# Chunk-selected attention with a gated feed-forward: query rows and their selection by DMA from the second pair on, two more engine choices, a shorter load count in the planner, and new ranks

## The chip, the cores and the metric

The kernel runs on one core of one Trainium2 chip. The metric is device microseconds per execution. For the kernel before it is the median of three runs, 320.1 us (319.93 to 320.34). The chip's engines each run their own instruction queue in order: TensorE (PE, with PEld for its weight loads), VectorE (DVE), ScalarE (ACT), GpSimd (POOL), and SyncE (SP), which here only issues DMAs.

## The reference

Inputs q, k, v have shape (4, 8, 768, 64) in fp32. Keys fall into 24 chunks of 32. For each query an upper bound of its score against each chunk is computed from the chunk's minimum and maximum, the six best causal chunks are kept, and attention runs over those alone. The result, as 3072 rows of 512, goes through a normalised SwiGLU feed-forward (512 to 1536 to 512).

```python
k_min = np.min(k_chunks, axis=3);  k_max = np.max(k_chunks, axis=3)
ub = np.sum(np.maximum(q[:, :, :, None, :] * k_min[:, :, None, :, :],
                       q[:, :, :, None, :] * k_max[:, :, None, :, :]), axis=-1)
ub = np.where(causal, ub, -1000000000.0)
top_chunks = np.argsort(ub, axis=-1)[..., -top_k:]             # top_k = 6
...
scores = np.where(mask, scale * np.matmul(q, k.transpose(0, 1, 3, 2)), -1000000000.0)
attn = softmax(scores)                                          # then attn @ v
...
rms = np.sqrt(np.mean(x * x, axis=-1, keepdims=True) + 1e-06)
xn = x / rms * rms_g
g = xn @ w_gate
return (g * (1.0 / (1.0 + np.exp(-g))) * (xn @ w_val)) @ w_out
```

## The kernel before, in words

The unit of the attention part is a pair of heads: 16 pairs, four to a batch (`for p in range(NPAIRS)`). For a pair, `prep` loads keys and queries (`kload`, `qload`, line 504, on SP), turns them so that the head dimension lies on partitions (`kT`, `qT`, TensorE in fp32, line 526), copies them out of PSUM (`kE`, `qE`), takes each chunk's maximum and minimum (`kmx`, `kmn`, VectorE, lines 552 and 554) and their difference (`dif`, line 633), rectifies the queries (`relu`, line 666), and forms the bounds (`ub`, line 684). The bounds are copied out, turned back (`up`, line 708), masked (`ubm`), and the eight largest of each row are found (`max`, line 729). `pick` (step `sel`) then writes 24 flags and an offset per query and head. Flags and queries together are the right operand of the score matmul, QS, where rows 0 to 63 of one head are the queries and rows 64 on the selection; KE holds keys and a fixed pattern E, so one matmul gives scores in which unselected chunks are pushed far down.

QS is filled in one of two ways, by the constant `QM`. For pairs below `QM` (0 to 3 before), the turned queries are cast into QS (`qC`, two casts of 64x768), `pick` writes a tile `selq` with two instructions (lines 748 and 753), TensorE turns it (`selT`, line 768, six matmuls), and two copies bring it out of PSUM (`selC`). For pairs from `QM` on (`side_q`), the untransposed queries are cast into a row tile QN (`qN`, one cast of 128x768), `pick` writes the flags into the same tile with two instructions for each head (lines 739 and 742), and two DMA transposes on SP carry the whole into QS (`qX`, line 563). There are two QN tiles (`qn=2`). Scores (line 831), exponentials (line 848) and the product with v (line 867) follow in groups; every score matmul waits for the whole selection of its pair.

When all four pairs of a batch are done, `norm` takes each half batch, three row blocks of 128 at a time: sums of squares, an inverse root on GpSimd, and a scaling of each row block (`xs`, line 944, VectorE). Batch 0 is then turned on TensorE (`tp`, line 966), the other batches by DMA transposes (line 955). `ffn` runs gate (line 1000), value (1021) and output (1041) matmuls on TensorE with tanh on ScalarE and two products on VectorE.

The order of all this is written by a planner, `Order.run`, before the kernel is built. Every piece of work is a step with an estimated duration for each engine that may do it. At each moment of planned time a free engine takes the ready step with the lowest rank, provided that its buffers are free. Ranks are sums from two tables: `RANK` (per kind, for batch 0 and for later ones) and `TIMES` (per pair or stage: `a` for preparation, `l` for loads, `s` for scores, `n` for norms, `f` for the feed-forward). A step with bytes to load is taken to arrive when the planned DMA has moved everything before it at `RATE` bytes per us, plus 1.5 us; loads are held back while the planned DMA is over 3 us behind. The resulting lists are fixed; at run time the engines follow them in order and wait on semaphores.

TensorE's idle time in the beginning is filled with matmuls on zeros: 48 of 512 columns from the start (`BUSY`) and 40 of 256 columns after pair 2's scores (`LATER`), as steps with rank 1000 and more (line 345):

```python
for i in range(BUSY):
    bank = Buf("ps")
    add("busy", "PE", pe(4 * P), 1000.0 + i, busy(bank, 4 * P), [c_zero], opens=[bank])
```

`ROWS` and (after) `KSIDE` equal 16, the number of pairs, so the branches that they guard for the keys run in neither kernel.

Of the kernel before, what the change touches and what calls it, by code (L numbers as in the profile page):

```python
# [8 lines left out]
FP32 = mybir.dt.float32  # L9
# [18 lines left out]
        av=132.14, dif=-438.04, eps=7.54, exp=-319.11, kC=334.22, kE=136.01, kT=-485.02,  # L28
        kload=-54.57, kmn=-137.23, kmx=-301.52, max=-152.41, qC=109.54, qE=316.44, qT=171.34,
        qload=-51.07, relu=59.75, root=77.15, sc=154.73, sel=83.19, selC=291.06, selT=-117.97,  # L30
        sq=-378.33, tp=24.59, tpE=360.56, ub=-188.41, ubE=-631.05, ubm=-71.86, up=-402.33,
        vload=-29.64, xb=-262.2, xs=247.58,
    ),
    dict(
        av=-265.86, dif=4.6, eps=-792.39, exp=258.27, gate=4.29, hh=-241.0, kC=134.04,
        kE=332.01, kT=-79.45, kload=194.09, kmn=455.81, kmx=359.92, mask=48.28, max=274.06,
        out=-113.88, po=207.1, poE=221.55, qE=-270.87, qN=298.48, qT=-27.26, qX=-362.48,
        qload=199.51, relu=279.63, root=-878.4, sc=-37.49, sel=336.13, sq=111.91, tanh=315.81,
        tg=61.58, ub=88.65, ubE=-137.69, ubm=107.32, up=172.52, val=34.42, vload=256.19,
        xT=-70.38, xb=-239.74, xs=-343.95,  # L40
# [38 lines left out]
class Order:  # L79
    RATE = 0.2e6  # L80
# [17 lines left out]
    def run(self, places):  # L98
# [20 lines left out]
        while len(out) < len(self.steps):  # L119
# [6 lines left out]
            for e in free:  # L126
# [3 lines left out]
                for s in waiting[e]:  # L130
# [71 lines left out]
def kernel(  # L202
# [78 lines left out]
    def act(n):  # L281
        return 0.065 + n * 0.00083
# [113 lines left out]
    if ROWS < B * NP:  # L396
# [89 lines left out]
    def prep(c, i0, nb, at, lr):  # L486
# [6 lines left out]
        done, ready = {}, {}  # L493
        rows_k, side_q = p >= ROWS, p >= QM
        for w, src in (("k", k), ("q", q)):
# [20 lines left out]
            if w == "k" and rows_k:  # L516
                continue

            evs = []
            for j0 in range(0, nb, 3):  # L520
                bank = Buf("ps", "prep")

                def turn(e, w=w, j0=j0, bank=bank):
                    t = tile_of(bank, [P, 3 * P], FP32, "p" + w)
                    for j in range(3):
# [5 lines left out]
                         opens=[bank], uses=[nat[w]])  # L531

# [38 lines left out]
        if rows_k:  # L571
            kh, km, kt = Buf("kh"), Buf("km"), Buf("ps", "prep")

            def load_h(e):
                t = tile_of(kh, [QC, 2, CH // 4, D], FP32, "khalf")
                for h in range(2):
                    nc.sync.dma_start(out=t[:, h], in_=k[b, h0 + h].rearrange(
                        "(c t) d -> c t d", t=CH // 4))

            ldh = add("khload", "SP", 1.4, rank(lr, b, "khload"), load_h, opens=[kh], load=220000)  # L580

            def whole(e, which):
                op = ALU.min if which else ALU.max
                if not which:
                    tile_of(km, [QC, 2, CH // 8, D], FP32, "kmm")
                to, src = (kh if which else km).tile, kh.tile
                m = CH // 8
                while m:
                    nc.vector.tensor_tensor(out=to[:, :, 0:m], in0=src[:, :, 0:m],
                                            in1=src[:, :, m:2 * m], op=op)  # L590
                    src, m = to, m // 2

            w_x = add("kmx", "DVE", 1.15, rank(at, b, "kmx"), lambda e: whole(e, 0), [ldh], opens=[km],
                      uses=[kh])
            w_n = add("kmn", "DVE", 1.15, rank(at, b, "kmn"), lambda e: whole(e, 1), [w_x], uses=[kh])

            def turn_m(e):
                t = tile_of(kt, [P, 2, QC], FP32, "kmt")
                for m, x in ((0, km), (1, kh)):
                    nc.tensor.transpose(t[:, m], x.tile[:, :, 0, :], ident_f[0:QC, 0:QC])  # L600

            tmt = add("kT", "PE", 0.19, rank(at, b, "kT"), turn_m, [w_x, w_n, c_id], opens=[kt],
                      uses=[km, kh])

            def join(e):
                tile_of(mx, [P, NCH], FP32, "kmx")
                for m in range(2):
                    nc.vector.tensor_reduce(
                        out=KU[c.ku.slot][:, 0, 0:NCH] if m else mx.tile[:],
                        in_=kt.tile[:, m].rearrange("p (c t) -> p c t", t=4),  # L610
                        axis=AXX, op=ALU.min if m else ALU.max)

            reds.append(add("join", "DVE", 0.44, rank(at, b, "join"), join, [tmt] + c_ku,
                            opens=[mx, c.ku], uses=[kt]))
# [27 lines left out]
        for w, dst in (("k", KE), ("q", QS)):  # L642
            if rows_k if w == "k" else side_q:
                continue
# [19 lines left out]
        def relu(e):  # L664
            t = tile_of(rel, [P, S], FP32, "rt")
            nc.vector.tensor_scalar(out=t[:, 0:n], in0=big["q"].tile[:, 0:n], scalar1=0.0,
                                    scalar2=None, op0=ALU.max)
# [436 lines left out]
```

## Time and profile before

| | |
|---|---|
| median of 3 runs | 320.1 us (319.93 to 320.34) |
| the profiled execution | 320.69 us, span 319.0 us, granted TensorE clock 0.998 |
| TensorE busy | 312.6 us, 98% of the span |
| VectorE, ScalarE, GpSimd busy | 237.2 (74%), 189.7 (59%), 105.1 (33%) us |
| DMA | 34.98 MB moved, 110 GB/s over the span |

The span runs from the first instruction to the last. Busy time is a sum over instructions and says nothing of which one ends last; the chain of waits, followed back from the last instruction, does. Matmul ends are modelled, so a busy TensorE may still contain short waits. Line numbers (L768) are those of the kernel before.

### The profile page before, as it was taken

The numbers are of one execution on the slowest core, as the hardware profiler recorded it, in microseconds if no ns is written. First come the engines' busy times: TensorE is split into PE (matmuls) and PEld (weight loads), VectorE is DVE, ScalarE is ACT, GpSimd is POOL, SyncE is SP. The second block draws the span as 40 slices with busy tenths as digits, with TensorE's granted clock in tenths as the row PEclk, the third lists the DMA queues.
The fourth block names the chain that finished last, engine by engine and source line by source line (L and its number), as shares of the span: only waits on it lengthen the run. The fifth ranks groups of instructions, "written<-read, shape, count | busy, mean of one in ns | idle before, by whom it ended". The sixth has DMA issues, their size and how long they took to land.

```text
span 319.0 us, 7874 instructions
## 1 busy us (share of the span) xinstructions
PE 312.6 (98%) x2922; PEld 199.6 (63%) x2940; DVE 237.2 (74%) x684; ACT 189.7 (59%) x418; POOL 105.1 (33%) x155
## 2 busy tenths in 40 slices
PE   8999999999999999999999999999999999999995
PEld 4576887666657767775657665567666566555542
DVE  7787988999965798999997968674677978716300
ACT  4478988553318888996348465469777343323121
POOL 8768345540003647496026135114211100000000
PEclk9999999999999999999999999999999999999999
DMA  9999994899929998959973414572000430001022
GB/s 174 218 208 176 201 126 78 107 201 170 69 65 213 211 184 192 165 126 205 78 112 85 46 28 55 121 170 82 16 2 2 83 84 0 2 33 66 35 89 109
DMA packets 111702, 34.98 MB, mean 110 GB/s; under 512 B 104624, under 2 KB 108464, under 8 KB 111664
## 3 DMA queue, kind: packets, MB, share of 16 engines
q1 hardware_dynamic: 81552, 26.23, 40.2%
q0 software_dynamic: 28512, 7.87, 26.3%
q10 hardware_dynamic: 1600, 0.39, 0.6%
q8 instruction: 23, 0.38, 0.5%
q14 instruction: 15, 0.12, 0.1%
HBM read 28.57 MB, written 6.29 MB: 109 GB/s over the span
## 4 chain that ended last, share of the span: by engine, by line
PE 96%; DVE 2%; issue 1%; ACT 0%; ACTq 0%; DVEq 0%
PE vp L1021 20%; PE gp L1000 20%; PE po L1041 19%; PE sc L831 11%; PE av L867 6%; PE ub L684 5%; PE busy L345 5%; PE pk L526 4%; PE pq L526 3%; PE up L708 2%; PE sc L837 1%; PE st L768 0%; PE tp L966 0%; DVE kmx L552 0%; DVE qs L300 0%
## 5 line engine op out<-in xcount | busy, mean ns | idle before, releaser
L848 ACT ACTIVATE pt<-sc 128x512 bf16<-128x512 f32 (+3 forms) x192 | 90.1, 583 | 10.4 <-PE sc L831 8.2
L1007 ACT ACTIVATE sg<-gp 128x384 bf16<-128x384 f32 x96 | 47.3, 497 | 62.9 <-PE gp L1000 61.3
L1021 PE MATMUL vp<-xT,wv 128*128 128x384 bf16 x384 | 75.8, 326 | 0.1
L1000 PE MATMUL gp<-xT,wg 128*128 128x384 bf16 x384 | 75.2, 326 | 0.0
L1013 DVE SCALAR_TENSOR_TENSOR tg<-sg,gp 128x384 bf16<-128x384 bf16 x96 | 51.7, 549 | 23.7 <-ACT sg L1007 22.2
L1041 PE MATMUL po<-wo,hh 128*128 128x512 bf16 x272 | 66.7, 379 | 0.8
L1029 DVE TENSOR_TENSOR hh<-vp,tg 128x384 bf16<-128x384 f32 x96 | 52.1, 552 | 14.0 <-PE vp L1021 12.4
L831 PE MATMUL sc<-qs,ke 89*128 89x128 bf16 (+5 forms) x420 | 53.3, 251 | 0.1
L1021 PEld LDWEIGHTS <-wv 128*128 128x128 bf16 x384 | 36.6, 98 | 24.7 <-issue 0.4
L1000 PEld LDWEIGHTS <-wg 128*128 128x128 bf16 x384 | 36.6, 98 | 23.3
L1041 PEld LDWEIGHTS <-hh 128*128 128x128 bf16 x288 | 27.5, 98 | 28.5 <-issue 0.4
L854 POOL TENSOR_SCALAR_AFFINE_SELECT pt<-pt 128x512 bf16<-128x512 bf16 (+1 forms) x48 | 25.4, 544 | 55.2 <-ACT pt L848 55.1
L867 PEld LDWEIGHTS <-pt 128*128 128x128 bf16 x672 | 31.4, 98 | 10.7 <-issue 2.1
L867 PE MATMUL av<-vx,pt 128*128 128x65 bf16 x672 | 36.7, 194 | 0.0
L831 PEld LDWEIGHTS <-ke 89*128 89x128 bf16 (+1 forms) x420 | 30.0, 97 | 9.2 <-issue 1.4
L300 POOL CAST ke<-kt 64x768 bf16<-64x768 f32 x31 | 27.7, 895 | 14.3 <-ACT kt L296 8.1
L298 ACT ACTIVATE osb<-po 128x512 f32<-128x512 f32 x21 | 12.7, 605 | 29.3 <-PE po L1041 29.2
L345 PE MATMUL busy<-zeros 128*128 128x512 bf16 (+1 forms) x86 | 20.5, 355 | 1.4 <-DVE zeros L340 1.3
L888 DVE TENSOR_TENSOR xb<-av,rden 128x384 bf16<-128x384 f32 (+1 forms) x34 | 18.1, 534 | 1.2
L944 DVE SCALAR_TENSOR_TENSOR xs<-xb,ri,gains 128x512 bf16<-128x512 bf16 x24 | 17.6, 766 | 1.7 <-DMA xT<-xs 1.7
L729 DVE MAX8 m<-ubm 128x8 f32<-128x24 f32 x192 | 18.7, 169 | 0.1
L633 POOL TENSOR_TENSOR ku<-kmx,ku 128x24 f32<-128x24 f32 x9 | 3.2, 357 | 45.4 <-DVE ku L554 42.8
(77 smaller groups left out, 322.3 us busy)
## 6 DMA issues: line engine op xcount, KB each, us to landing
out_dram<-osb SPq DMA_DIRECT2D x24, 256.0 KB, 2.2
knat<-in_k_dram SPq DMA_DIRECT2D x30, 192.0 KB, 4.4
qnat<-in_q_dram SPq DMA_DIRECT2D x30, 192.0 KB, 4.3
vx<-in_v_dram POOLq DMA_DIRECT2D x16, 192.0 KB, 7.1
wg<-in_moe_w_gate_dram POOLq DMA_DIRECT2D x2, 768.0 KB, 7.2
wv<-in_moe_w_val_dram POOLq DMA_DIRECT2D x2, 768.0 KB, 7.4
wo<-in_moe_w_out_dram POOLq DMA_DIRECT2D x2, 768.0 KB, 12.9
ke<-e_all SPq DMA_DIRECT2D x4, 96.0 KB, 3.7
```

The lines of the kernel that those rows point to most:

```text
L300: engine[e].tensor_copy(out_, in_)
L345: nc.tensor.matmul(t[:, 0:n], zeros[:, 0:P], zeros[:, 0:n], start=True, stop=True)
L831: nc.tensor.matmul(t[:, x:x + m, :].rearrange("p a b -> p (a b)"), ke[kk, kb * P:(kb + 1) * P], qs[kk, q0 * P:(q0 + m) * P], start=not tri ...
L848: nc.scalar.activation(out=t[:, 0:nn, :], in_=sc.tile[:, 0:nn, :], func=ACT.Exp, scale=SCALE)
L854: nc.gpsimd.affine_select(out=pt.tile[:, 0:nd, :], in_=pt.tile[:, 0:nd, :], compare_op=ALU.is_ge, fill=0.0, base=0, pattern=[[0, nd], [1, ...
L867: nc.tensor.matmul(av.tile[:, qi - i0, :], pt.tile[:, x, :], VX[c.v.slot][:, hl * NT + kb, :], start=(begin and m == 0), stop=(left[0] == ...
L1000: nc.tensor.matmul(t[:], wg[:, g, hs], XT[b].tile[:, g, cols], start=(g == 0), stop=(g == NP - 1))
L1007: nc.scalar.activation(out=t[:], in_=gp.tile[:], func=ACT.Tanh, scale=0.5)
L1013: nc.vector.scalar_tensor_tensor(out=t[:], in0=sg.tile[:], scalar=1.0, in1=gp.tile[:], op0=ALU.add, op1=ALU.mult)
L1021: nc.tensor.matmul(t[:], wv[:, g, hs], XT[b].tile[:, g, cols], start=(g == 0), stop=(g == NP - 1))
L1029: nc.vector.tensor_tensor(out=t[:], in0=vp.tile[:], in1=tg.tile[:], op=ALU.mult)
L1041: nc.tensor.matmul(po.tile[:], hhs[ht].tile[:, th * P:(th + 1) * P], wo[:, ht, :], start=(ht == 0), stop=(ht == NHT - 1))
```

## The change

Five things change together.

- `QM` goes from 4 to 1: pairs 1, 2 and 3 fill QS by the row tile and the DMA transposes, as pairs 4 to 15 already do. One `selq` tile is left of two.
- The planner may put `relu` on ScalarE as well as on VectorE.
- The planner may put `xs` on GpSimd as well as on VectorE; there it is two instructions with an fp32 tile between them. One hidden tile fewer is kept (`hh` 33 to 32).
- The planner's `RATE` goes from 0.2e6 to 0.25e6 bytes per us, and only loads over 250,000 bytes are held back.
- All values of `RANK` and `TIMES` are new.

The unused branch for keys is also written differently. The core of the diff:

```diff
 RANK = (
     dict(
-        av=132.14, dif=-438.04, eps=7.54, exp=-319.11, kC=334.22, kE=136.01, kT=-485.02,
+        av=-194.02, dif=128.57, eps=135.49, exp=-30.2, kC=211.42, kE=-32.81, kT=-200.58,
...
 TIMES = {
-    "a0": -499.17, "a1": -82.98, "a10": 213.54, "a11": 202.23, "a12": 347.75, "a13": 367.65,
+    "a0": 166.8, "a1": 73.35, "a10": 214.63, "a11": -67.16, "a12": 163.94, "a13": 312.87, "a14":
...
 class Order:
-    RATE = 0.2e6
+    RATE = 0.25e6
...
-                    if s.load and dma > t + 3.0:
+                    if s.load > 250000 and dma > t + 3.0:
                         heapq.heappush(events, dma - 3.0)
                         continue
...
-    ROWS, QM, SEL2 = 16, 4, 0.42
-    QC, HW = S // (CH // 4), NT * P + D
+    KSIDE, QM, SEL2 = 16, 1, 0.42
+    HW = NT * P + D
...
-    SLOTS = dict(ps=8, nat=7, kh=1, km=1, kb=0, qn=2, vext=4, set=3, ku=3, selq=2, qt=7, ubs=2, small=8, ubm=3,
-                 pt=10, xb=2, xt=2, row=3, xs=4, ff=8, hh=33, ob=3)
+    SLOTS = dict(ps=8, nat=7, kb=0, qn=2, vext=4, set=3, ku=3, selq=1, qt=7, ubs=2, small=8, ubm=3,
+                 pt=10, xb=2, xt=2, row=3, xs=4, ff=8, hh=32, ob=3)
...
         def relu(e):
             t = tile_of(rel, [P, S], FP32, "rt")
-            nc.vector.tensor_scalar(out=t[:, 0:n], in0=big["q"].tile[:, 0:n], scalar1=0.0,
-                                    scalar2=None, op0=ALU.max)
-
-        rl = add("relu", "DVE", 0.07 + n * 0.00056, rank(at, b, "relu"), relu, done["q"], opens=[rel],
+            if e == "ACT":
+                nc.scalar.activation(out=t[:, 0:n], in_=big["q"].tile[:, 0:n], func=ACT.Relu)
+            else:
+                nc.vector.tensor_scalar(out=t[:, 0:n], in0=big["q"].tile[:, 0:n], scalar1=0.0,
+                                        scalar2=None, op0=ALU.max)
+
+        rl = add("relu", "", {"DVE": 0.07 + n * 0.00056, "ACT": act(n)}, rank(at, b, "relu"), relu, done["q"], opens=[rel],
                  uses=[big["q"]], port=True)
...
             def scale(e, j=j, i=i, xs=xs):
                 t = tile_of(xs, [P, DM], BF16, "xs")
+                if e == "POOL":
+                    f = sb.tile([P, DM], FP32, name="xf", tag="xf")
+                    nc.gpsimd.tensor_scalar(out=f[:], in0=XB[b].tile[:, i, :], scalar1=rt.tile[:, j:j + 1],
+                                            scalar2=None, op0=ALU.mult)
+                    nc.gpsimd.tensor_tensor(out=t[:], in0=f[:], in1=gains[:], op=ALU.mult)
+                    return
...
-            x = add("xs", "DVE", 0.67, rank(at, b, "xs", j, pace), scale, [r, c_gain], opens=[xs],
+            x = add("xs", "", {"DVE": 0.67, "POOL": 1.35}, rank(at, b, "xs", j, pace), scale, [r, c_gain], opens=[xs],
                     uses=[XB[b], rt], port=True)
```

More of the change, by code (lines that the diff above doesn't have):

```diff
@@ L27 @@
     dict(
-        av=132.14, dif=-438.04, eps=7.54, exp=-319.11, kC=334.22, kE=136.01, kT=-485.02,
[L29 to L32, printed above, removed]
+        av=-194.02, dif=128.57, eps=135.49, exp=-30.2, kC=211.42, kE=-32.81, kT=-200.58,
+        kload=-56.92, kmn=138.83, kmx=-214.94, max=-121.99, qC=-64.94, qE=80.5, qN=-155.22,
+        qT=125.3, qX=-464.87, qload=-55.33, relu=54.97, root=82.86, sc=78.08, sel=-103.77,
+        selC=-123.83, selT=39.9, sq=-38.85, tp=27.84, tpE=-161.42, ub=16.24, ubE=-12.11,
+        ubm=34.91, up=-45.2, vload=-91.36, xb=123.33, xs=194.99,
     ),
     dict(
[L35 to L40, printed above, removed]
+        av=-0.69, dif=-82.23, eps=99.49, exp=34.36, gate=-20.02, hh=-151.12, kC=213.59,
+        kE=108.14, kT=-9.96, kload=-8.3, kmn=-38.66, kmx=1.9, mask=151.72, max=82.0, out=201.96,
+        po=49.59, poE=74.31, qE=-232.27, qN=3.53, qT=0.49, qX=-277.65, qload=-7.17, relu=-80.37,
+        root=-77.21, sc=22.16, sel=-4.96, sq=105.84, tanh=-255.68, tg=-113.66, ub=-57.0,
+        ubE=153.74, ubm=-146.54, up=-29.23, val=-11.61, vload=187.07, xT=101.12, xb=137.85,
+        xs=-15.06,
     ),
@@ L395 @@
     c_kb = []
-    if ROWS < B * NP:
+    if KSIDE < B * NP:
         et = Buf("ps", "prep")
@@ L492, in prep @@
         nat, big = {}, {}
-        done, ready = {}, {}
-        rows_k, side_q = p >= ROWS, p >= QM
+        done, ready, kbanks = {}, {}, []
+        side_k, side_q = p >= KSIDE, p >= QM
         for w, src in (("k", k), ("q", q)):
@@ L515, in prep @@
             ready[w] = ld
-            if w == "k" and rows_k:
-                continue
             evs = []
@@ L531, in prep @@
                          opens=[bank], uses=[nat[w]])
+                if w == "k" and side_k:
+                    kbanks.append((j0, bank, tr))
+                    continue
                 def out_(e, w=w, j0=j0, bank=bank):
@@ L570, in prep @@
         reds, casts = [], []
[L571 to L614, printed above, removed]
@@ new lines, in prep, with red2 @@
+        if side_k:
+            def red2(e, which, j0, bank):
+                a0, a1 = j0 * 4, (j0 + 3) * 4
+                if which == 0 and mx.tile is None:
+                    tile_of(mx, [P, NCH], FP32, "kmx")
+                nc.vector.tensor_reduce(
+                    out=KU[c.ku.slot][:, 0, a0:a1] if which else mx.tile[:, a0:a1],
+                    in_=bank.tile[:].rearrange("p (c t) -> p c t", t=CH), axis=AXX,
+                    op=ALU.min if which else ALU.max)
+            for j0, bank, tr in kbanks:
+                reds += [add("kmx", "DVE", 0.07 + 3 * P * 0.00106, rank(at, b, "kmx", j0, "step"),
+                             lambda e, j0=j0, bank=bank: red2(e, 0, j0, bank), [tr], opens=[mx], uses=[bank]),
+                         add("kmn", "DVE", 0.07 + 3 * P * 0.00106, rank(at, b, "kmn", j0, "step"),
+                             lambda e, j0=j0, bank=bank: red2(e, 1, j0, bank), [tr] + c_ku,
+                             opens=[c.ku], uses=[bank])]
@@ L642, in prep @@
         for w, dst in (("k", KE), ("q", QS)):
-            if rows_k if w == "k" else side_q:
+            if side_k if w == "k" else side_q:
                 continue
```

28 rows, old and new, of the table TIMES are left out of this document.

## The prediction

> **What bounds the kernel now.** I read the page first: engine shares, then the chain that ended last.
>
> ```profile
> PE 312.6 (98%) x2922; PEld 199.6 (63%) x2940; DVE 237.2 (74%) x684; ACT 189.7 (59%) x418; POOL 105.1 (33%) x155
> ...
> PE 96%; DVE 2%; issue 1%; ACT 0%; ACTq 0%; DVEq 0%
> ```
>
> TensorE carries 96% of the chain. Next I asked for stages (columns: stretch, its length, busy time and count of PE, PEld, DVE, ACT, POOL, granted clock, DMA share, GB/s), and then for the filler matmuls alone (line 345, stages from 0 to 80 us).
>
> ```profile
> 20.00:30.00 10.00, 9.91 (x138) 6.83 (x143) 8.68 (x22) 9.35 (x21) 8.02 (x10) 1.00 1.23 189
> 30.00:40.00 10.00, 10.00 (x141) 8.06 (x130) 8.37 (x39) 9.06 (x22) 4.27 (x6) 1.00 1.39 190
> 40.00:50.00 10.00, 9.85 (x170) 7.68 (x171) 8.98 (x21) 8.86 (x21) 3.41 (x6) 1.00 0.99 145
> ...
> 56.00:80.00 24.00, 24.00 (x184) 15.45 (x183) 23.41 (x76) 11.13 (x24) 7.80 (x10) 1.00 1.33 160
> ```
> ```profile
> sum 80.00, PE 20.53 PEld 8.70; mean PE 2.93 PEld 1.24
> ```
>
> From 56 us on, where the first gate matmul stands on the chain,
>
> ```profile
> 56.40 1.95 PE gp L1000 x12
> ```
>
> TensorE is full of real work. Before that it looks full too, but 20.5 us of what it does there are matmuls on zeros. These 88 fillers (48 + 40 in the code) are steps of the list like any other: every one is issued, with the change as without. So the change cannot win by "needing fewer fillers"; TensorE's total falls only by real work taken away, and any wait that the new order adds comes on top. The clock is 1.00 throughout, so it gives nothing.
>
> In one place the chain leaves TensorE for VectorE, at the fourth pair's selection (chain in order of time: start, us, what):
>
> ```profile
> 40.25 0.35 PE st L768 x6
> 40.60 0.02 issue
> 40.63 0.56 DVE qs L300
> 41.19 0.01 issue
> 41.20 0.55 DVE qs L300
> 41.75 0.34 DVE kmx L552
> ```
>
> This is exactly what the change replaces: six transposes of the selection on TensorE and two copies out of PSUM.
>
> **The change part by part.** The sum is made against the profiled execution: span 319.0, its own time 320.69, so 1.69 us lie around the span. The median shown, 320.1, is 0.59 lower; I carry the sum over to it.
>
> (1) Selection of pairs 1 to 3, rows of the old path and then of the new one (median is the middle number, ns):
>
> ```profile
> L768 PE MATMUL st<-ident_b,selq x24: 217/219/220, 18.1 to 40.4; 128*128 128x128 bf16 x24
> L748 DVE SCALAR_TENSOR_TENSOR selq<-m,ubm x4: 442/446/809, 17.2 to 38.1; 128x288 bf16<-128x288 f32 x4
> L753 DVE TENSOR_SCALAR selq<-m x4: 184/325/821, 17.5 to 38.8; 128x12 bf16<-128x12 f32 x4
> ```
> ```profile
> L739 DVE SCALAR_TENSOR_TENSOR qn<-m,ubm x24: 289/300/314, 78.8 to 214.1; 128x144 bf16<-128x144 f32 x24
> L742 DVE TENSOR_SCALAR qn<-m x24: 172/174/385, 79.0 to 214.3; 128x6 bf16<-128x6 f32 x24
> L563 SPq DMA_TRANSPOSE qs<-qn x24: 1210/1236/1971, 79.7 to 221.8; - x24
> L300 POOL CAST qn<-qnat x8: 812/822/1132, 29.5 to 212.0; 128x768 bf16<-128x768 f32 x8
> ...
> DMA to landing us min/median/max: 2.5/2.7/5.3
> ```
> ```profile
> L300 POOL CAST qs<-qt x7: 814/826/1221, 8.7 to 26.4; 64x768 bf16<-64x768 f32 x7
> L296 ACT ACTIVATE qs<-st x4: 803/804/805, 18.7 to 28.0; 64x768 bf16<-64x768 bf16 x4
> L300 DVE COPY qs<-st x4: 549/555/561, 35.8 to 41.2; 64x768 bf16<-64x768 bf16 x4
> ```
>
> TensorE loses 3 x 0.35 us (the chain's piece for six transposes) = 1.05 us, all on the path: **-1.05**. GpSimd loses six casts and gains three: 6 x 0.826 - 3 x 0.822 = 2.5 us free, off the path. ScalarE loses one pair of copies, 1.6 us; VectorE loses two pairs, 2.2 us, and its selection grows from 0.446 + 0.325 to 2 x (0.300 + 0.174), +0.18 a pair, so 1.7 us net.
>
> The latency goes the other way. For the fourth pair, from the end of line 753 to the first score matmul on line 831:
>
> ```profile
> 38.82 0.46 DVE L753 TENSOR_SCALAR selq<-m 128x12 bf16<-128x12 f32 x1
> ...
> 41.97 0.50 PE L831 MATMUL sc<-qs,ke 128*128 128x128 bf16 x6
> ```
>
> That is 41.97 - 39.28 = 2.7 us. The new link: one issue ahead (1.24), then the second transpose's landing, 2.7 at the median, 5.3 at most: 3.9 to 6.5 us, +1.2 to +3.8. Every score of a pair needs both transposes. The place is 40 us into the kernel, with the DMA share near 1; loads there land late:
>
> ```profile
> DMA packets 25247, 5.96 MB, mean 198 GB/s; under 512 B 25034, under 2 KB 25113, under 8 KB 25241
> ...
> qnat<-in_q_dram SPq DMA_DIRECT2D x12, 192.0 KB, 5.8
> ```
>
> (the DMA view of 10 to 40 us.) So I take the upper half: **+2.4** for the fourth pair, whose link stands on the chain. The second and third pairs have other pairs' work behind them and I cost them at nothing; without that cover, each costs the same again. The ends, +1.2 and +3.8, stay for the range.
>
> (2) Loads counted shorter. The planner now takes a key or query load (two issues of 192 KB, 393,216 bytes, entered as 422,400) at 422,400 / 0.25e6 = 1.69 us where it took 2.11; the chip moved 198 GB/s, so 1.99 us. The order was a little cautious and becomes 0.30 us a load optimistic; engines run it in order, so a transpose placed for an early arrival stands and everything behind it on TensorE waits. Six loads for pairs 1 to 3: between 0 and 1.8 us; I take half, **+0.9**. That loads under 250,000 no longer wait in the plan moves small issues earlier on SP; rows exist for none, and I leave it inside the second rival.
>
> (3) Rectified queries on ScalarE. Nearest rows: the same step on VectorE, a ScalarE pass over 768 columns, and the table load.
>
> ```profile
> L666 DVE TENSOR_SCALAR rt<-qt 128x768 f32<-128x768 f32 x16 | 9.4, 592 | 0.4 <-ACT qt L296 0.4
> ...
> L337 ACT ACT_TABLE_LOAD x1 | 1.3, 1283 | 3.0 <-issue 3.0
> ...
> L296 ACT ACTIVATE ke<-kt 64x768 bf16<-64x768 f32 x1 | 0.8, 841 | 0.0
> ```
>
> 0.84 on ScalarE for 0.59 on VectorE: in the early stage ScalarE is at 89 to 94%, VectorE at 84 to 90, so what moves there gains nothing; later ScalarE has room and TensorE is full. **0**, from -0.5 to +0.8 (three early ones at 0.84 less 0.59). One load of tables serves exponential, tanh and square in this trace; were the rectifier outside that set, each use would cost two loads, 2.57 us. The Trainium skill ("ScalarE: Activation LUTs", Table sets) says that cheap functions, relu among them, stand in every set; by that the cost is none, and no run so far shows it.
>
> (4) Norm rows on GpSimd. One fused VectorE instruction becomes two on GpSimd, the second with two inputs.
>
> ```profile
> L944 DVE SCALAR_TENSOR_TENSOR xs<-xb,ri,gains 128x512 bf16<-128x512 bf16 x24 | 17.6, 766 | 1.7 <-DMA xT<-xs 1.7
> ...
> L854 POOL TENSOR_SCALAR_AFFINE_SELECT pt<-pt 128x512 bf16<-128x512 bf16 x24 | 15.6, 650 | 47.8 <-ACT pt L848 47.7
> ...
> L633 POOL TENSOR_TENSOR ku<-kmx,ku 128x24 f32<-128x24 f32 x9 | 3.2, 357 | 45.4 <-DVE ku L554 42.8
> ...
> L633 DVE TENSOR_TENSOR ku<-kmx,ku 128x24 f32<-128x24 f32 x7 | 1.7, 240 | 0.0
> ```
>
> Below: two passes like line 854's, 1.30 us. Above: two VectorE passes scaled by line 633's ratio, 2 x 0.766 x 357/240 = 2.28. Planned: 1.35. I take 1.8, nearer to the upper end since two inputs are read. Three rows go on VectorE one after another ahead of the first feed-forward (3 x 0.766 = 2.3 us). With one on GpSimd the set ends at about 1.8, 0.5 earlier; with two, at 3.6, 1.3 later; with all, at 5.4, 3.1 later. Only the first set is bare, later ones lie beside a full TensorE: **+0.4**, from -0.5 to +3.1. The Trainium skill ("GPSIMD Engine Reference", Elementwise side by side) speaks against this edit: it has a two-input add at 4497 ns there against 2293 on VectorE for 2048 elements. By its figures the pair of instructions is an estimated 1.9 us and the sum 0.1 us higher; the trace shows no such instruction.
>
> (5) Relief and ranks. ScalarE and VectorE lose 1.6 and 1.7 us in the stage where both run near 90%, worth at most the larger, and VectorE stands on the chain from 40.63 us on: from -1.7 to 0, **-0.5**, since the two copies on the chain are already replaced in (1). The new ranks redo every engine's order; no row prices that. TensorE's share leaves little to gain from 56 us on and much to lose; I count it at 0 and let it widen the range. One spare hidden tile fewer (33 to 32) and one selection buffer fewer: 0, as one pair alone still uses the latter.
>
> Sum: -1.05 + 2.4 + 0.9 + 0 + 0.4 - 0.5 = +2.15 us. 320.69 + 2.15 = 322.84 for a profiled run, **322.3** for the median. Its own range is 321.0 to 325.5.
>
> **The rivals.** *Early relief decides.* If the rest of the order keeps the fourth pair off the end of the early stage (its scores behind other pairs' exponentials), the DMA link is hidden, and 1.05 us of TensorE and about 2 us of VectorE and ScalarE come off: 320.1 - 3.1 = 317.0. For it: both engines near 90%, and VectorE's place on the chain. Against it: fillers are fixed and the stage's loads saturate the DMA. It decides once the link's added 2.4 us find that much other TensorE work.
>
> *SP's queue becomes the bound.* SP issues without pause early; first and last rows of thirteen groups:
>
> ```profile
> 9.08 1.26 SPq L504 DMA_DIRECT2D knat<-in_k_dram  x2
> ...
> 34.66 3.53 SPq L504 DMA_DIRECT2D qnat<-in_q_dram  x2
> ```
>
> Six transposes add 6 x 1.24 = 7.4 us to these 29, and each stands until its selection is done, with the loads of pairs 4 to 6 behind it; both row buffers are then held till landing, and GpSimd's next layout waits with masks and casts behind it. If that runs through to TensorE: 320.1 - 1.05 + 7.4 = about 326.5. Against: those pairs are not needed before the first norm.
>
> *It comes out even:* the link's lower end (+1.2) against -1.05, the rest cancelling: 320.2. *A table load per rectifier:* three early ones, 7.7 us on ScalarE: 327.8.
>
> **How the numbers follow.** Forecast 0.46, relief 0.28, SP queue 0.15, even 0.09, table load 0.02. Slower by over 0.2% (0.64 us, about what can be told from no change): 0.63; within: 0.09; faster: 0.28. The range, 316.5 to 327.5, reaches from below the relief case to past the queue case; the ranks are its largest unknown.
>
> **What would show it.** Right: no line 768 after the first pair, three more pairs of query transposes before 60 us, landing 4 to 6 us; the chain passing through a query transpose or a load; the first gate matmul 1 to 4 us after 56.4; filler count 88 unchanged. GpSimd norm rows at 1.6 to 2.0 us the pair. One table load. Wrong: the first gate earlier than 56 us with TensorE idle no larger than now, or idle appearing behind 80 us, where I put none.

## The result, and the profile after

The changed kernel takes 335.92 us (median of six runs, 331.54 to 338.35); the kernel before took 320.22 us beside it. The ratio is 1.0445, 95% interval [1.0382, 1.0509], which is 14.2 us of 320.2 (12.2 to 16.3); it is one of means and leaves out the two longest of the six runs, so it is smaller than that of the medians. It is slower, and by far more than the 2.15 us that I had forecast. Below, each kernel is compared by its ratio, and "us" is (ratio - 1) x 320.2.

The page of the changed kernel (profiled at 335.32 us, span 333.6, granted clock 0.99), engine shares and the chain that ended last:

```profile
PE 317.5 (95%) x2922; PEld 200.5 (60%) x2922; DVE 226.8 (68%) x657; ACT 198.3 (59%) x429; POOL 141.3 (42%) x181
...
PE 73%; DMA 17%; POOL 5%; SPq 1%; issue 1%; DVE 1%; ACT 1%; ACTq 0%; DVEq 0%; POOLq 0%
```

TensorE carried 96% of the chain; now it is 73%, and DMA and GpSimd hold 22%. The span is 14.6 us longer and TensorE is busy only 4.9 us longer, so some 10 us are new idle time. The windows of the changed kernel show where (stretch, length, busy time and count of PE, PEld, DVE, ACT, POOL, granted clock, DMA share, GB/s):

```profile
10.00:20.00 10.00, 8.23 (x87) 4.51 (x85) 6.93 (x25) 3.66 (x7) 6.73 (x11) 1.00 1.37 209
...
30.00:40.00 10.00, 9.20 (x149) 6.61 (x148) 7.26 (x28) 8.96 (x21) 3.74 (x6) 1.00 1.00 144
...
50.00:60.00 10.00, 6.43 (x57) 4.92 (x55) 4.40 (x11) 4.92 (x10) 5.29 (x5) 0.73 1.26 209
56.00:80.00 24.00, 24.00 (x208) 17.05 (x206) 17.74 (x53) 17.76 (x41) 16.83 (x18) 0.89 1.01 180
80.00:100.00 20.00, 17.69 (x144) 11.37 (x143) 18.49 (x55) 9.61 (x22) 6.20 (x10) 1.00 1.61 142
100.00:130.00 30.00, 27.25 (x401) 19.94 (x399) 22.11 (x71) 24.02 (x56) 19.71 (x28) 1.00 1.29 157
```

Two holes stand out: 3.6 us at 50 to 60 us, and 2.3 us at 80 to 100 us, the second where I had put none. Before the change TensorE was busy for 10.00 and 19.95 us of these two stretches. Two more are as large: 1.8 us at 10 to 20 us, most of it a wait for a key load (1.4 us), and 2.8 us at 100 to 130 us, waits for v loads. Before, TensorE was busy for 9.94 and 29.78 us there. The chain of the changed kernel up to 110 us, in order of time (start, us, what), its larger DMA and GpSimd pieces from 23 us on and the first gate matmuls:

```profile
23.53 9.67 DMA qs<-qn
...
43.76 11.09 DMA qs<-qn
...
62.54 1.30 PE gp L982 x8
...
70.45 1.57 POOL xf L922
...
78.18 0.43 POOL xs L924
...
79.39 6.91 DMA wv<-in_moe_w_val_dram
86.30 14.68 DMA qs<-qn
...
101.88 5.48 DMA vx<-in_v_dram
```

The reader is to see three query transposes of 10 to 15 us, and a value weight load that starts only when GpSimd has finished its norm rows: at 79.39 us. The kernel before issued it at 60.74, on GpSimd's timeline:

```profile
60.74 0.90 POOL L444 DMA_DIRECT2D wv<-in_moe_w_val_dram  x1
```

The first gate matmul stands 6.1 us later than the 56.40 of before. SP's own timeline in the changed kernel (start, length of the group, count), and below it one line of the kernel before:

```profile
21.79 26.84 SPq L564 DMA_TRANSPOSE qs<-qn  x8
48.68 3.79 SPq L504 DMA_DIRECT2D knat<-in_k_dram  x2
```
```profile
22.28 1.65 SPq L504 DMA_DIRECT2D knat<-in_k_dram  x2
```

Eight transposes, of pairs 2, 1, 3 and also 5. Pair 5 is of the second batch; before the change its first transpose was issued at 79.67 us. The new ranks have put it here, and its scores ahead of the first norm's transposes on TensorE's list. Behind the eight stand the loads of the sixth pair in order of issue, from 48.68 us on; before the change the sixth pair's were issued from 22.28 us on.

The instructions of the other parts (duration ns min/median/max, first and last start, shape) and the landing of the transposes:

```profile
L564 SPq DMA_TRANSPOSE qs<-qn x30: 1210/1239/4867, 21.8 to 252.5; - x30
...
DMA to landing us min/median/max: 2.5/4.5/14.7
```
```profile
L922 POOL TENSOR_SCALAR xf<-xb,ri x14: 1564/1568/2655, 51.3 to 279.9; 128x512 f32<-128x512 bf16 x14
L924 POOL TENSOR_TENSOR xs<-xf,gains x14: 1262/1274/1512, 53.6 to 281.5; 128x512 bf16<-128x512 f32 x14
...
L640 ACT ACTIVATE rt<-qt x12: 837/844/912, 12.7 to 243.3; 128x768 f32<-128x768 f32 x12
```

Landing was 2.5/2.7/5.3 before. A norm row on GpSimd takes 2.84 us at the medians, 3.05 at the means (1.749 + 1.300).

### The profile page after: what moved, and what is told of

The parts are those of the page before. It is cut to its first block, busy times and chain, and to the rows that moved or that the text cites. A ratio compares the mean times of both kernels' runs of the same rounds, so it can differ in the third digit from the quotient of the medians.

```text
span 333.6 us, 7891 instructions
## 1 busy us (share of the span) xinstructions
PE 317.5 (95%) x2922; PEld 200.5 (60%) x2922; DVE 226.8 (68%) x657; ACT 198.3 (59%) x429; POOL 141.3 (42%) x181
## 4 chain that ended last, share of the span: by engine, by line
PE 73%; DMA 17%; POOL 5%; SPq 1%; issue 1%; DVE 1%; ACT 1%; ACTq 0%; DVEq 0%; POOLq 0%
PE po L1023 18%; PE vp L1003 15%; PE gp L982 15%; DMA qs<-qn 11%; PE sc L807 9%; PE av L843 5%; DMA knat<-in_k_dram 3%; PE ub L660 3%; PE busy L345 3%; POOL xf L922 2%; DMA wv<-in_moe_w_val_dram 2%; PE pk L524 2%; PE pq L524 2%; DMA vx<-in_v_dram 2%; POOL xs L924 1%; PE up L684 1%
## 5 line engine op out<-in xcount | busy, mean ns | idle before, releaser
L824 ACT ACTIVATE pt<-sc 128x512 bf16<-128x512 f32 (+1 forms) x192 | 89.2, 576 | 15.0 <-PE sc L807 11.9
L982 PE MATMUL gp<-xT,wg 128*128 128x384 bf16 x384 | 77.5, 326 | 0.0
L1023 PE MATMUL po<-wo,hh 128*128 128x512 bf16 x288 | 70.3, 379 | 0.0
L807 PE MATMUL sc<-qs,ke 89*128 89x128 bf16 (+5 forms) x420 | 56.1, 256 | 4.4 <-DMA qs<-qn 4.2
L843 PE MATMUL av<-vx,pt 128*128 128x65 bf16 x672 | 38.7, 194 | 4.0 <-DMA vx<-in_v_dram 2.8
L843 PEld LDWEIGHTS <-pt 128*128 128x128 bf16 x672 | 32.3, 98 | 15.7 <-issue 3.0
L300 POOL CAST ke<-kt 64x768 bf16<-64x768 f32 x31 | 25.9, 837 | 26.6 <-ACT kt L296 14.7
L922 POOL TENSOR_SCALAR xf<-xb,ri 128x512 f32<-128x512 bf16 x14 | 24.5, 1749 | 1.1
L924 POOL TENSOR_TENSOR xs<-xf,gains 128x512 bf16<-128x512 f32 x14 | 18.2, 1300 | 1.2
L480 POOL DMA_DIRECT2D vx<-in_v_dram x16 | 17.0, 1066 | 3.8 <-PE av L843 3.5
```

The lines of the kernel that those rows point to most:

```text
L300: engine[e].tensor_copy(out_, in_)
L807: nc.tensor.matmul(t[:, x:x + m, :].rearrange("p a b -> p (a b)"), ke[kk, kb * P:(kb + 1) * P], qs[kk, q0 * P:(q0 + m) * P], start=not tri ...
L824: nc.scalar.activation(out=t[:, 0:nn, :], in_=sc.tile[:, 0:nn, :], func=ACT.Exp, scale=SCALE)
L843: nc.tensor.matmul(av.tile[:, qi - i0, :], pt.tile[:, x, :], VX[c.v.slot][:, hl * NT + kb, :], start=(begin and m == 0), stop=(left[0] == ...
L922: nc.gpsimd.tensor_scalar(out=f[:], in0=XB[b].tile[:, i, :], scalar1=rt.tile[:, j:j + 1], scalar2=None, op0=ALU.mult)
L982: nc.tensor.matmul(t[:], wg[:, g, hs], XT[b].tile[:, g, cols], start=(g == 0), stop=(g == NP - 1))
```

## The experiments

Most of these kernels keep the planned order of one of the two kernels and alter single steps in it, so that the order is the same on both sides of each comparison.

| kernel | ratio to before | 95% interval | us |
|---|---|---|---|
| changed kernel | 1.0445 | 1.0382 to 1.0509 | +14.2 |
| changed, norm rows on VectorE | 1.0379 | 1.0354 to 1.0404 | +12.1 |
| changed, thin weight loads | 1.0136 | 1.0094 to 1.0179 | +4.4 |
| changed, thin loads and norm rows on VectorE | 1.0061 | 1.0038 to 1.0083 | +2.0 |
| changed, rectified queries on VectorE | 1.0424 | 1.0369 to 1.0479 | +13.6 |
| changed, pair 5 turned on TensorE | 1.0400 | 1.0354 to 1.0446 | +12.8 |
| changed, pairs 1, 2, 3, 5 turned on TensorE | 1.0441 | 1.0408 to 1.0474 | +14.1 |
| the same, and norm rows on VectorE | 1.0249 | 1.0211 to 1.0287 | +8.0 |
| before, thin weight loads | 1.0013 | 0.9995 to 1.0030 | +0.4 |
| before, pairs 1 to 3 selected by DMA | 1.0352 | 1.0299 to 1.0405 | +11.3 |
| the same, thin weight loads | 1.0281 | 1.0241 to 1.0320 | +9.0 |
| before, one rectified query on ScalarE | 1.0000 | 0.9971 to 1.0028 | 0.0 |
| before, without the 40 later fillers | 0.9949 | 0.9926 to 0.9972 | -1.6 |

**Norm rows back on VectorE.**

```diff
-        s.emit(s.eng)
+        s.emit("DVE" if s.name == "xs" else s.eng)
```

> The changed kernel with its lists as they are, but every norm row (the scaling by root and gains) on VectorE at its place in the order. Changed kernel: 335.9 us; GpSimd norm rows there are 14 pairs of 1.75 + 1.30 us, and six instructions in a row from 70.4 us stand ahead of the second value-weight load, issued at 79.4 where the kernel before issued it at 60.7. If these rows delay that load and what hangs on it (theory B), the load goes out near 71 us, the TensorE gap at 84 to 88 us closes and the time falls by 4 to 6 us, to 330 to 332. If the loss is DMA transposes that land late behind weight and value loads (theory A), it falls by under 2 us: 334 to 336. If the lists are poor as such (theory C): within 1 us of 335.9.

Measured 332.86 us. The second value load on GpSimd's timeline comes 8.8 us earlier, and TensorE's busy time in 80 to 100 us rises from 17.69 to 19.80:

```profile
70.57 0.80 POOL L444 DMA_DIRECT2D wv<-in_moe_w_val_dram  x1
```

So the second hole is GpSimd's, but it is not the large term: +12.1 stay. The two intervals overlap, and the size of this part alone is uncertain.

**Thin weight loads**, in both kernels: each of the six loads brings one tile of 128 columns or rows instead of six, and all matmuls use it. Five sixths of the weights are left out; every matmul, wait and step is as before.

```diff
-        cols = slice(part * (DFF // 2), (part + 1) * (DFF // 2))
+        cols = slice(part * (DFF // 2), part * (DFF // 2) + P)
```

In the changed kernel:

> The changed kernel, same lists, but each of the six weight loads moves one hidden tile of 128 columns (or rows) in place of six, and all matmuls of that half use this one tile: the weights are left out to five sixths, the instructions stay. The six loads then move 1.6 MB in place of 9.4. Theory A: the transposes issued at 42.2 and 43.8 us land in 3 to 5 us in place of 11 to 12, those at 84.9 and 86.3 in 3 to 5 in place of 10 to 15; the first gate matmul comes near 55 us in place of 62.5 and the time falls by 8 to 12 us, to 324 to 328. Theory B alone: the late value load lands at once, 330 to 332. Theory C: 334 or more.

In the kernel before:

> The kernel before with the same thin weight loads (five sixths of each weight left out, the one loaded tile used for all), as the control for the run on the changed kernel. It has no DMA transpose before 79.7 us, when the weights have all but landed. Theory A: it falls by 0 to 1.5 us, to 318.7 to 320.2, so that the thin loads are worth 8 or more only where transposes stand among them. If thin loads speed up any list by as much (loads, not transposes), it falls by 5 or more.

Measured 324.8 and 320.67 us. The kernel before does not mind its weight traffic; the changed one gives back 9.8 us without it. Some 3 of these are the clock: it is granted at 0.73 over 50 to 60 us in the changed kernel and at 1.00 with thin loads (see the last section). The first gate matmul, on TensorE's timeline of the changed kernel with thin loads:

```profile
57.47 0.81 PE L984 MATMUL gp<-xT,wg 128*128 128x384 bf16 x4
```

With the norm rows on VectorE as well:

> The changed kernel, same lists, with both cures at once: thin weight loads (five sixths of each weight left out, as before) and every norm row on VectorE. Alone they came to 324.8 (thin) and 332.9 us (rows). Theory A and B as one: the rows on GpSimd hurt only by delaying the second value load, which a thin load makes good, so together no more than thin alone: 324 to 325.5. If GpSimd's rows cost by their own length too (TensorE waited 0.8 us for such a row in the thin run, and masks and casts stand behind them), 321 to 323.

Measured 322.22 us: +2.0 is all that is left for everything else in the change. In its profile TensorE waits directly for transposes only 0.4 us in all, and longest for a query load (us in total, times, longest):

```profile
PE pq L525 <- DMA qnat<-in_q_dram: 2.2, 1, 2.2
```

**The first part alone.** The order of the kernel before, with pairs 1 to 3 laid out in row tiles and turned by DMA at the place of the six matmuls (a third row tile lies in `wo`, which is not loaded yet).

```diff
+        dq = 1 <= p < QM
...
+            if dq:
+                for hl in range(2):
+                    nc.sync.dma_start_transpose(
+                        out=QS[c.set.slot][hl][:].rearrange("d (t p) -> d t p", p=P),
+                        in_=QD[p][:, hl * HW:hl * HW + NT * P])
+                return
```

> The kernel before with its lists, but pairs 1 to 3 fill the query operand by row tile and two DMA transposes each, at the places of the old steps: one cast in place of two, flags written for each head, the transposes on SP where TensorE turned the flags, and nothing for that turn and the copies out. One more row tile lies in the memory of the output weights, which are loaded later. This is the first part of the change alone. The prediction's step: -1.05 us of TensorE, +1.2 to +3.8 at the fourth pair, so 320.2 to 323, with relief down to 318.5. Theory A: no weight load stands ahead of these six transposes before 38.5 us, so they land in 4 to 7 us and the time is 319 to 323. Theory D, that DMA transposes early cost most of the loss wherever they stand: 328 or more.

Measured 331.89 us, far above what I expected: +11.3 us with no new rank, norm row or rectifier in it. Its chain of waits, then what TensorE waited for directly (us in total, times, longest):

```profile
27.77 4.22 DMA qs<-qn
...
43.73 7.47 DMA qs<-wo
...
65.30 1.95 PE gp L1019 x12
```
```profile
PE sc L850 <- DMA qs<-qn: 6.4, 2, 3.7
PE sc L850 <- DMA qs<-wo: 1.9, 1, 1.9
```

TensorE waits at all three pairs, 8.3 us in sum, and the first gate matmul is 8.9 us late. The clock adds to it (0.83 over 40 to 50 us, so some 1.7 us of full-speed work):

```profile
40.00:50.00 10.00, 6.57 (x45) 4.50 (x45) 4.28 (x11) 6.35 (x14) 4.77 (x6) 0.83 1.09 129
```

The same with thin weights:

> The kernel before with pairs 1 to 3 filled by DMA transposes (331.9 us with whole weights), now with thin weight loads (five sixths left out). Theory A: the last pair's transposes, issued at 42.5 us just behind a weight load at 41.7, land in 3 to 4 us in place of 8, which is worth 4 to 5 us: 326 to 328. If the loss of that kernel is mostly the weights' traffic: 320 to 323. If it is the transposes' own length three times over on a chain with nothing beside it (theory D), with SP's later loads standing behind them: 329 to 332.

Measured 329.27 us, +9.0. Its chain still goes through the transposes:

```profile
27.62 5.15 DMA qs<-qn
...
45.95 3.01 DMA qs<-wo
```

In this order the weights make about 2.3 of the 11.3 us (the two intervals overlap). The rest is the link, taken three times in a row, with what it holds up on SP's queue and in the clock.

**The transposes by themselves.** A small kernel without the computation: two transposes of a 128x768 tile on SP, started by a short GpSimd copy, alone or behind one, two or three weight loads of 1.57 MB on GpSimd's queue, or behind four key and query loads on SP's; then the two norm-row instructions on GpSimd, alone and beside VectorE.

> Not the task: a kernel that only measures (all of the computation is left out, zeros are written). Three times over: two DMA transposes of 128x768 on SP with nothing else in flight, then behind one, two and three weight loads of 1.57 MB from GpSimd's queue, then behind four key or query loads on SP's own queue; then norm rows on GpSimd alone and beside VectorE. Theory A: landing 2.5 to 3 us alone, and some 5, 10 and 14 us or more behind one, two, three weight loads, near the time that the loads themselves need at 200 GB/s (8 us each). Rival: transposes share the engines with the loads from the first packet on, and land within 6 us whatever stands ahead. GpSimd: 1.75 and 1.30 us beside VectorE; alone the first is 0.6 to 1.0 if the rest is waiting for the shared port.

Its GpSimd timeline gives the start (the copy into `src`), VectorE's the first read of the result:

```profile
59.99 0.18 POOL L68 COPY src<-fence 128x2 bf16<-128x2 bf16 x1
65.91 0.20 POOL L68 COPY src<-fence 128x2 bf16<-128x2 bf16 x1
76.52 0.20 POOL L68 COPY src<-fence 128x2 bf16<-128x2 bf16 x1
91.72 0.22 POOL L68 COPY src<-fence 128x2 bf16<-128x2 bf16 x1
```
```profile
63.04 0.17 DVE L72 COPY fence<-dst 128x2 bf16<-128x2 bf16 x1 [3.42 <-DMA dst<-src]
73.46 0.17 DVE L72 COPY fence<-dst 128x2 bf16<-128x2 bf16 x1 [8.86 <-DMA dst<-src]
87.42 0.17 DVE L72 COPY fence<-dst 128x2 bf16<-128x2 bf16 x1 [12.94 <-DMA dst<-src]
103.86 0.17 DVE L72 COPY fence<-dst 128x2 bf16<-128x2 bf16 x1 [14.92 <-DMA dst<-src]
```

From copy to first read: 2.9 us alone, 7.4 behind one load, 10.7 behind two, 11.9 behind three. The 9.67, 11.09 and 14.68 us of the changed kernel's chain are of this size: there the first stands among v loads and, from 31.33 us on, a gate load, the second behind a gate and a value load, the third behind both output loads, as the second value load lands. Behind four loads on SP's own queue it was 4.2 us (from 109.92, where SP's group of transposes starts, to a first read at 114.13). The norm-row instructions:

```profile
L86 POOL TENSOR_SCALAR xf<-xb,rt x14: 1562/1875/1881, 172.5 to 215.8; 128x512 f32<-128x512 bf16 x14
```
```profile
L87 POOL TENSOR_TENSOR xs<-xf,gains x14: 1260/1488/1490, 174.2 to 217.8; 128x512 bf16<-128x512 f32 x14
```

Six pairs ran alone (1.56 + 1.26 = 2.82 us), eight beside VectorE (1.88 + 1.49 = 3.36): so most of their length is their own, and no wait.

**Which transposes hold the first norm in the changed order.** First I turned the selection of pairs 1 to 3 on TensorE again, in the changed kernel's order:

```diff
+                if name == "qX" and p in PEQ:      # (1, 2, 3) here; then (5,) and (1, 2, 3, 5)
+                    ...
+                    for j in range(nb):
+                        nc.tensor.transpose(t[:, j * P:(j + 1) * P], SELP[:, j]..., ident_b[:])
```

> The changed kernel's lists, but pairs 1 to 3 fill QS as before: casts on GpSimd, selection turned by six matmuls on TensorE at the place where their transposes stood, two copies out (ScalarE and VectorE). Pair 5 keeps its DMA transposes among the weight loads. Theory 1 (the late transposes of pairs 1 to 3 are a large term in these lists as well): 326 to 331 us, and the chain has no query transpose before 40 us. Rival (in these lists the loads and the order, with pair 5's transposes ahead of the first norm, hold the first gate anyway): 333 to 336 us, the first gate matmul still at 61 to 63 us behind a query transpose issued near 43 us.

In this kernel one selection tile served pair 0 too, so that pair 0 attends to pair 2's chunks; the steps and waits are those named. Measured 334.02 us, ratio 1.0418 [1.0350, 1.0486] (a variant that turns at the second of the two places, in another PSUM bank: 334.82, 1.044). The chain shows why nothing moved:

```profile
46.71 9.77 DMA qs<-qn
...
61.19 1.35 PE gp L1007 x8
```

The pieces are those of pair 5, the only early pair left on DMA. Three more kernels, with a selection tile of their own, separated the pairs:

> The changed kernel's lists; pair 5's selection alone is turned on TensorE, pairs 1 to 3 keep their DMA transposes. If pair 5's transposes, put ahead of the first norm by the new ranks, hold the first gate matmul: 330 to 333 us, first gate 58 to 60 us. If those of pairs 1 to 3 hold it as much: 334 to 336 us, first gate 61 us or later.

> The changed kernel's lists; the selection of pairs 1, 2, 3 and 5 is turned on TensorE, as before the change it was for pairs 0 to 3. Theory A (the query transposes among the weight loads, pair 5's last, hold the first gate matmul): it goes from 62.5 to 57 to 59 us, and the time to 329 to 332 us. Theory B (the new order holds it by itself, and any late piece takes the transposes' place): 333 to 336 us, first gate 61 us or later. The late transposes near 85 us and the second value load stay in both.

> As the run with pairs 1, 2, 3 and 5 turned on TensorE, and every norm row on VectorE. By theory A the two gains add up (about -5 and -3): 326 to 329 us, and what is left stands behind 80 us at the transposes that queue behind the value and output weights. By theory B: 331 to 333 us, as with the norm rows alone.

Measured 334.05, 334.41 and 328.67 us. The first gate matmul came 3.1 us earlier with pair 5 alone on TensorE (59.41, as expected if pair 5 holds it) and 2.1 us earlier with all four (60.39, later than theory A's 57 to 59). Yet the times of both, +12.8 and +14.1 us, can't be told from the changed kernel's: theory A's 330 to 333 and 329 to 332 us were missed. The chain of the kernel with pairs 1, 2, 3 and 5 on TensorE, and its window of 80 to 100 us:

```profile
60.39 1.30 PE gp L1011 x8
...
77.26 7.21 DMA wv<-in_moe_w_val_dram
84.52 0.82 PE vp L1032 x4
```
```profile
80.00:100.00 20.00, 17.93 (x129) 10.87 (x127) 16.83 (x51) 8.16 (x19) 6.39 (x10) 0.91 1.28 146
```

The earlier start lasts until the second half of the value weights: TensorE begins with these at 84.52 us here and at 83.78 with pair 5 alone, against 86.92 in the changed kernel. All three wait about as long for them (2.1, 2.3 and 2.3 us), so the gain is not lost in the wait. Behind it the clock is granted at 0.91 over 80 to 100 us in these two kernels, 20 x 0.09 = 1.8 us of full-speed work, and at 1.00 in the changed kernel. The profiled executions end up 1.5 and 2.2 us shorter than its own, which is less than these few runs can tell. Pair 5's kernel also waits 4.0 us for query loads, the changed kernel 0.3.

Where the norm rows are on VectorE as well, the load goes out at 68.93, TensorE does not wait for it (20.00 us busy of 80 to 100, clock 1.00), and the earlier gain counts: -4.1 us against the norm rows alone (12.1 to 8.0), and -6.1 against the transposes alone (14.1 to 8.0). What is left lies further back in its chain:

```profile
84.89 10.39 DMA qs<-qn
96.17 5.94 DMA vx<-in_v_dram
```

**The remaining parts.** Rectified queries on VectorE, in the changed kernel's order:

> The changed kernel's lists, with all 16 rectified queries on VectorE (12 of them were on ScalarE at 0.85 us). Theory: this part cost nothing and gained nothing: 335 to 337 us. Rival (ScalarE's longer pass stands on the way of the early pairs, or VectorE was relieved): 332 to 334, or above 338 us.

Measured 334.22 us, 1.0424 [1.0369, 1.0479]: no difference that can be told. The reverse, one of them on ScalarE in the kernel before (the sixth, which stood on its chain):

> The kernel before, with one rectified query, the sixth, on ScalarE (the one that stands on the chain at 43.86 us with 0.54 us on VectorE). If VectorE's place on the chain near 41 to 44 us is what sets the first norm: 319.5 to 320.0 us. If TensorE's own list takes its place at once: 320.0 to 320.5 us, no difference that can be told.

Measured 320.16 us, ratio 1.0000 [0.9971, 1.0028]: nothing. Last, the fillers, in the kernel before:

```diff
+        if s.name == "busy" and s.occ["PE"] < 0.15:
+            continue
```

> The kernel before without the 40 filler matmuls that stand after pair 2's scores (4.4 us of TensorE; they are left out, and the result doesn't depend on them). If the fillers stand on the path, as I argued (all are issued, so they count in full): 316 to 318 us. If they only fill waits: 319.9 to 320.5 us. If they hold the clock: a granted clock below 1.00 somewhere between 40 and 60 us and 321 us or more.

Measured 318.99 us, 1.6 us faster than before (0.9 to 2.4), the only kernel here that beats both. Its windows where the fillers stood:

```profile
40.00:50.00 10.00, 9.12 (x159) 6.89 (x163) 9.20 (x21) 9.11 (x23) 3.35 (x6) 1.00 0.98 145
50.00:60.00 10.00, 8.74 (x95) 6.05 (x84) 9.51 (x23) 8.29 (x20) 5.98 (x7) 1.00 0.45 63
```

It came out between my two cases: of 4.4 us of filler matmuls some 1.6 were on the path, and the rest filled time in which TensorE has nothing else. The clock held at 1.00 with gaps this short.

## Why the prediction was wrong, by its own steps

**Right in direction, wrong in size and in the main term.** The chain does pass through query transposes and a load, as the forecast said; 335.9 is outside the range's 327.5. Of the signs that I named, the first gate matmul came 6.1 us after 56.4 where I had said 1 to 4, and idle time behind 80 us, my sign of being wrong, is there.

- *Step (1), the price of the link.* This step failed by itself: its terms make -1.05 + 2.4 = +1.35 us, and the first part alone measured +11.3. I bounded the link's landing by 5.3 us, the longest of 24 transposes (and +2.4, which I called the upper half, is just under the middle of 1.2 and 3.8). All of those rows start at 79.7 us or later, after the last weight load's issue at 61.64. The early ones stand beside v and weight loads, and took up to 11.9 us (14.7 later on). I had seen that loads land late there (5.8 us) and used it only to choose within the old bound. The row was the right operation in the wrong company.
- *The cover of the second and third pairs.* "Other pairs' work behind them, at nothing" fell with the first part alone: TensorE waited at all three pairs. My fallback, the same price for each, makes 3 x 2.4 - 1.05 = 6.2 us; measured +11.3, or +9.0 with thin weights. I had counted three priced links as independent, but each also held SP's queue: in that kernel the loads issued before at 25.56 to 34.66 us came at 46.96 and after. How much of the 9.0 is this and how much the link was not separated. That kernel's order was planned for the old path; in the new order TensorE's direct waits for transposes are 4.2 us, 3.6 of them for pair 5.
- *The new ranks, "at 0".* In the changed kernel this is the step that failed most, as far as the runs tell. The ranks moved pair 5's transposes among the weight loads and ahead of the first norm, GpSimd's casts and norm rows ahead of the second value load, and the output loads next to later transposes. With pairs 1, 2, 3 and 5 back on TensorE and the norm rows back on VectorE, +8.0 us stay for the ranks, the load count and the copies which that kernel needs on top (the rectified queries cost nothing). Through weight traffic the new order and its transposes lose 9.8 us, the old order with the same first part some 2.3. No run has the new ranks without the other parts, so their own share stays open. A rank moves loads too, so an unpriced new order deserved a case of its own with a long tail, not a widened range.
- *Step (4), norm rows.* I took 1.8 us a row from bounds of 1.30 and 2.28; measured 3.05. Both bounds scaled other shapes: line 854's 0.650 us is one pass on bf16 in and out, and the fp32-writing first pass alone takes 1.56. The Trainium skill ("GPSIMD Engine Reference", Elementwise side by side), by which I had estimated 1.9, is close for the two-input half (an estimated 4497/4 = 1.12 us for 512 elements; 1.26 to 1.30 here); it is the other half that no bound had. The place was wrong as well: not the bare first set (0.8 us of direct wait, in the kernel with thin loads) but the second, ahead of the value load on the same in-order engine. I had named VectorE's relief and not asked what else GpSimd issues.
- *Step (2), loads counted shorter.* TensorE's direct waits for keys and queries went from none to 1.7 us (1.4 and 0.3), within my 0 to 1.8. The other kernels with this order show 0.3 to 4.0, and 2.8 where thin loads and norm rows on VectorE leave +2.0, so that most of these 2.0 may be this step. Load count and ranks were not separated; that stays open.
- *Step (3), rectified queries.* Right: 0.84 us each, one table load, no effect on the time in either kernel. The rule of the Trainium skill ("ScalarE: Activation LUTs", Table sets) on relu agrees with the one load seen (1.28 us).
- *Step (5), relief.* -0.5 was not seen. VectorE fell from 237.2 to 226.8 us busy, and nothing of it shows in the time; TensorE then waited on DMA.
- *The clock, "it gives nothing".* It was a term of its own, put at nothing because the kernel before had no hole: some 3 us behind the hole at 50 to 60 us.
- *Fillers.* All 88 are issued, as said, but ten now stand at the very end beside the last output, and not all cost their length: 40 of them cost 1.6 us of 4.4.
- *The second rival, SP's queue,* described the order of events (the sixth pair's loads at 48.68 instead of 22.28 us, behind the transposes) and had its price too low: it counted issue time, 7.4 us, where SP stands for 26.84 us over eight transposes. Its counter-argument, that those pairs are not needed before the first norm, was undone by the new ranks for pair 5.

**What adds up.** Of +14.2 us, thin weight loads remove 9.8, and norm rows on VectorE 2.4 more; 2.0 remain for the link without traffic, the load count and the order. The parts do not simply add: undoing the early transposes alone leaves 14.1, the norm rows alone 12.1, and both 8.0. The early transposes are worth some 4 us once the value load no longer comes late, and nothing that shows before.

## What to carry to other kernels

Price a moved DMA by rows that stand beside the same traffic as its new place; a landing measured on quiet queues is a lower bound. Before work goes to an engine "with room", list what that engine issues behind it, weight loads above all. When two gates stand in series, undo both before you call either one harmless, and look at the granted clock behind each hole.

## What the runs showed of the hardware

A DMA transpose on SP slows down with loads on another queue, 2.9 us alone to 11.9 behind three weight loads, nearly until these are done (the last load landed 7.4, 11.3 and 14.6 us after its issue with one, two and three). The Trainium skill ("DMA: Bandwidth & Descriptors", Queues, rings and completion order) has each DMA engine take turns between queues packet by packet; that would let small packets wait on large ones, but no run here tells turns from a plain queue.

A hole in TensorE's work costs more than itself. The changed kernel in short windows:

```profile
52.00:56.00 4.00, 1.10 (x13) 1.10 (x13) 1.13 (x2) 0.42 (x1) 2.74 (x2) 0.83 1.27 217
56.00:60.00 4.00, 4.00 (x28) 2.73 (x26) 1.85 (x6) 2.82 (x6) 1.01 (x2) 0.50 1.37 218
60.00:64.00 4.00, 4.00 (x34) 3.28 (x32) 0.34 (x2) 3.04 (x8) 0.51 (x1) 0.82 1.34 221
```

TensorE stands for 3.57 us ahead of 54.90. The clock is then granted at 0.50 for four microseconds and at 0.82 for the next four: 4 x 0.50 + 4 x 0.18 = 2.7 us of full-speed work lost, and up to 0.6 more in the 1.1 us of work that ends the first of these windows (0.83). Over the six runs of the changed kernel time and clock go together: 331.54 us at 0.995, 335.32 to 336.32 at 0.990, 336.95 and 338.35 at 0.985.

The Trainium skill ("TensorE: Matmul & The Clock Gate", Part 1) gives half rate after an idle window of about 3.4 us; this hole agrees. Shorter holes do not fit that sentence alone: behind the 2.1 us wait for value weights above the clock was granted at 0.91 over 80 to 100 us, behind the 2.3 us wait of the changed kernel at 1.00. What tells the two apart is not shown. "The clock gives nothing", as I wrote, holds only while nothing waits.
